# A convolution and squared-ReLU feed-forward kernel: new loads, a split first convolution and a new order in blocks 0 to 3

## The chip, the cores and the metric

One core of one Trainium2 chip. The metric is device time in microseconds (us) of one execution. The engines are called TensorE (PE in the profile; PEld is its weight load), VectorE (DVE), ScalarE (ACT), GpSimd (POOL) and SyncE (SP).

## The reference, cut to what matters

```python
# x: (8, 4096, 192), weight_gen: (8, 4096, 8 heads, 7 taps)
w = exp(weight_gen - max); w = w / sum(w)          # softmax over the 7 taps
out[b, s, head] = sum_k w[b, s, head, k] * x_pad[b, s + k, head]   # causal, 24 channels a head
h = maximum(out.reshape(32768, 192) @ w_in, 0)     # w_in (192, 2048)
return (h * h) @ w_out                             # w_out (2048, 192)
```

Everything is float32 outside; the kernel computes in float16 with float32 sums.

Of the kernel before, what the change touches and what calls it, by code (L numbers as in the profile page):

```python
# [9 lines left out]
def kernel(  # L10
# [7 lines left out]
):  # L18

# [38 lines left out]
    SL = 8  # L58
# [33 lines left out]
    mask = const.tile([P, P, 2], f16, name="mask")  # L92
    FIRST = 8
# [4 lines left out]
    ]  # L98

    def band_mask():  # L100

        nc.gpsimd.memset(mask, 1.0)
        for sign, base in ((1, 0), (-1, KK - 1)):
            nc.gpsimd.affine_select(
                out=mask, in_=mask, pattern=[[sign, P], [0, 2]], compare_op=AluOp.is_ge,
                fill=0.0, base=base, channel_multiplier=-sign,
            )

# [14 lines left out]

    def cross_w_in(q):
        for r0, r1 in ((0, RT), (RT, 0)):
            nc.sync.dma_start(out=w_i[r0 : r0 + RT, q, 1], in_=w_i[r1 : r1 + RT, q, 0])

# [10 lines left out]
    def load_w_out(q, n):  # L138
        nc.gpsimd.dma_start(
            out=w_o[:, q * NF // n : (q + 1) * NF // n],  # L140
            in_=moe_w_out[q * Dff // n : (q + 1) * Dff // n].rearrange(
                "(c p) m -> p c m", p=P
            ),
        )
# [139 lines left out]
    def x_load_f32(j):  # L284
        x_st[j] = p_one.tile([P, (R + HALO) * HK], f32, name="x_st", tag="ex")
        block_load(
            j, x_st[j][:, 0 : NT * D].rearrange("p (t d) -> p t d", t=NT), x[j // NBB], D, nc.sync
        )

    def x_cast(j, copy):  # L290
        x_t[j] = p_x.tile([P, NT, D], f16, name="xt")
        copy(out=x_t[j].rearrange("p t d -> p (t d)"), in_=x_st[j][:, 0 : NT * D])
# [6 lines left out]
    def wr_load_sbuf(j, parts, order, engines):  # L299

        wr_t[j] = p_wr.tile([P, NT, HP, SL * 2], f16, name="wr")
# [46 lines left out]
    def conv_pieces(j):  # L348


        s0, n = BLOCKS[j]
        th = n * TB // 2
        halves = []
        for half in (0, 1):
            s, a = (s0 + half, 0) if n == 2 else (s0, th * half)
            halves.append([
                (s, i, half, max(bounds[i], a), min(bounds[i + 1], a + th), a)
                for i in range(NT) if bounds[i] < a + th and bounds[i + 1] > a
            ])
        if n == 2:  # L360
# [14 lines left out]
    def st_conv(j):  # L375

        n = BLOCKS[j][1]
        th = n * TB // 2
        per = 1024 // th
        y = p_y.tile([P, NK, TB], f16, name="y")  # L380
        y_t[j] = y
# [3 lines left out]
        for later, s, i, q, half, a, b, base in conv_pieces(j):  # L385
# [7 lines left out]
            col = th * (k % per) - base  # L393
# [9 lines left out]
        for n, yp in enumerate(yps):  # L403
            k0, k1 = n * per, min((n + 1) * per, NK)
            nc.scalar.copy(  # L405
                out=y[:, k0:k1, 0:th],
                in_=yp[:, 0 : (k1 - k0) * th].rearrange("p (k c) -> p k c", c=th),
            )

    def st_unit(j, u):  # L410

        th = BLOCKS[j][1] * TB // 2
        per = TB // th
        h = ps_h.tile([P, 2, TB], f32, name="h", tag="h")
        for jj in range(per):
            for slot in range(NK):
                for half, r0 in enumerate((0, RT)):
                    k = slot ^ half if slot < 2 else slot
                    nc.tensor.matmul(  # L419
                        out=h[:, half, jj * th : (jj + 1) * th],  # L420
                        lhsT=w_in_chunk(u * per + jj, slot, half),
                        rhs=y_t[j][r0 : r0 + RT, k, 0:th],
                        start=(jj == 0 and slot == 0), stop=(slot == NK - 1),
                        skip_group_check=True,
                        tile_position=(r0, 0),
                    )
# [3 lines left out]
        g_t[(j, u)] = g  # L430
# [4 lines left out]
    def new_o(pool, banks=2):  # L435
        if pool is ps_o:
            return [ps_o.tile([P, TB], f32, name=f"o{i}") for i in range(banks)]
# [3 lines left out]
    def st_mm2(j, qt, fcs, ccs, o):  # L441


        th = BLOCKS[j][1] * TB // 2
        per = TB // th
        half, off = divmod(qt * QT, th)
        for fc in fcs:
            g = g_t[(j, fc // per)][:, half, fc % per * th + off :]
            for cc in ccs:
                n = P // len(o)  # L450
                for i, oo in enumerate(o):
# [3 lines left out]
                        lhsT=g[r0 : r0 + n, cc * P : (cc + 1) * P],  # L455
# [32 lines left out]
    with nc.allow_low_precision("fp16 matmul pipeline"), tc.manual_schedule():  # L488
# [18 lines left out]
        warm = const.tile([P, TB], f16, name="warm")  # L507
        nc.vector.memset(warm, 0.0)  # L508
# [3 lines left out]
        wp = ps_h.tile([P, 2 * TB], f32, name="wp", tag="h")  # L512

        def spin(n):
            for i in range(n):
                nc.tensor.matmul(  # L516
                    out=wp[:, 0:TB], lhsT=warm[:, 0:P], rhs=warm, start=True, stop=True
                )

        s0, s1, s2 = parts[:3]  # L520
        spin(42)
        band_mask()
        s0.load(nc.sync)
# [3 lines left out]
        ]  # L527
        load_w_in(w_st[0], 0, nc.sync)
        x_load_f32(0)
        load_w_in(w_st[1], 1, nc.sync)  # L530
        s0.exp(0, s0.rh)
# [3 lines left out]
        nc.scalar.copy(out=w_i[:, 0, 0], in_=w_st[0])  # L535
        wr_load_sbuf(0, [s0], (0, 2, 1, 4, 3), (nc.sync, nc.gpsimd))
        wr_load_sbuf(1, [s0], range(NT), (nc.gpsimd,))
        cross_w_in(0)
        x_cast(0, nc.scalar.copy)
        x_load_f32(1)  # L540
        nc.scalar.copy(out=w_i[:, 1, 0], in_=w_st[1])
        cross_w_in(1)
        s1.load(nc.sync)
        for i in (0, 2, 1, 3, 4):
            st_band(0, (i,))
        st_conv(0)
        st_bands(1)
        x_cast(1, nc.vector.tensor_copy)

        nc.gpsimd.memset(x_st[1][:, 0:1], 0.0)  # L550
# [3 lines left out]
        nc.gpsimd.memset(v_big, 0.0)  # L554
# [3 lines left out]
        orders = {0: "uuuuuCuuu", 1: "MuMuuuMuuuMCu", 2: "MuuuuMuuuuMuuuuuuuMCu"}  # L558
        steady = "MuMuuu" * 3 + "MuuuMCu"

# [4 lines left out]
        def at(j, u, kind, *args):  # L565
# [5 lines left out]
            (0, 2): ((1, 7), (2, 0)),  # L571
            (0, 3): ((2, 15), (3, 0)),
# [8 lines left out]
        def exp_time(j, u):  # L581

            if u == 0:
                return j - 1, 5 if j == 2 else 12
            return j, {1: 0, 7: 3, 9: 4, 15: 8}[u]

        at(0, 4, "exp", s1, 0, s1.rh)
        at(0, 5, "soft", s1, 0, s1.rh)
        for n, s in enumerate(parts[2:], 2):
# [5 lines left out]
            pieces = [(lo, min(lo + PIECE, s.rh)) for lo in range(0, s.rh, PIECE)]  # L595
            for (j, u), (lo, hi) in zip(times, pieces, strict=True):
                at(*exp_time(j, u), "exp", s, lo, hi)
                at(j, u, "soft", s, lo, hi)
            if n > 2:
                at(times[0][0] - 1, 0, "load", s)  # L600
        for j in range(1, NBLK - 1):
            a = BLOCKS[j + 1][0]
            small = [p for p in parts if p.fb <= j + 1][-1].r == FIRST
            us = {1: (1, 3), 2: (6, 8), 6: (7, 9)}.get(j, (5, 9) if small else (1, 5))
            for n, u in enumerate(us):
                at(j, u, "band", a + n)
# [14 lines left out]
        def run_fill(j, u):  # L621
            for kind, *args in fill.get((j, u), ()):
                if kind == "band":
                    st_bands(*args)
                    continue
                if kind == "load":
                    args[0].load(nc.sync)
                    continue
                s, lo, hi = args
                if kind == "exp":  # L630
                    s.exp(lo, hi)
                    continue
                s.total(lo, hi)
                s.recip(lo, hi)
                s.scale(lo, hi, nc.vector)
                if hi < s.rh:
                    continue
                if s.r == FIRST:
                    move_rows(s)
                    after = parts[parts.index(s) + 1]  # L640
                    if after.b == s.b and after.r > FIRST:
                        s.store(nc.sync)
                else:
                    s.store(nc.sync)
                    stored.add(s)
                    for w in [w for w in waiting if w[0] is s]:
                        waiting.remove(w)
                        load_rows(w[1])

        FCS = (range(NF // 2), range(NF // 2, NF))  # L650
        for j, (sub, n) in enumerate(BLOCKS):
            if j + 2 < NBLK:
                load_rows(j + 2)
            u = m = 0
            for step in orders.get(j, steady):
                if step == "M":
                    qt, part = divmod(m, 2)
                    m += 1
                    if part == 0:
                        o = new_o(ps_o, 1 if j < 3 else 2)  # L660
                    st_mm2(j - 1, qt, FCS[part], (0, 1), o)
                    if part == 1:
                        o_sum(j - 1, qt, (0, 1), o)
                        if qt % 2:
                            o_store(j - 1, qt - 1, range(4), nc.sync)
                elif step == "u":
                    run_fill(j, u)
                    st_unit(j, u)
                    u += 1
                elif j + 1 < NBLK:  # L670
                    st_conv(j + 1)
            if j == 0:
                x_load(2)
                x_load(3)
            elif j < NBLK - 2:
                for k in range(BLOCKS[j + 2][0], sum(BLOCKS[j + 2])):
                    x_load(k)
# [47 lines left out]
```

## The kernel before: what the change and the argument touch

The 32768 rows are worked through in blocks: two of 512 rows (blocks 0 and 1), then 31 of 1024. In each block the convolution is done on TensorE with banded weights `bd` (made by VectorE from softmax rows `wr` and a mask), ScalarE copies the result to `y`, 8 or 16 *units* follow (TensorE `h = w_in.T y`, ScalarE relu to `t`, VectorE square to `g`), and half-quarters *M* of the second product, four or eight a block, are placed between the units of the next block. A plan gives each block's order: `u` a unit, `M` a half-quarter, `C` the next block's convolution.

```python
orders = {0: "uuuuuCuuu", 1: "MuMuuuMuuuMCu", 2: "MuuuuMuuuuMuuuuuuuMCu"}
steady = "MuMuuu" * 3 + "MuuuMCu"
```

The start, shortened:

```python
spin(42)                                  # warm-up matmuls
s0.load(nc.sync)                          # softmax weights of the first 1024 rows
load_w_in(w_st[0], 0, nc.sync); x_load_f32(0); load_w_in(w_st[1], 1, nc.sync)
s0.exp(...); s0.total(...); s0.recip(...); s0.scale(...)
nc.scalar.copy(out=w_i[:, 0, 0], in_=w_st[0])           # cast of the first half of w_in
wr_load_sbuf(0, [s0], (0, 2, 1, 4, 3), (nc.sync, nc.gpsimd))   # band rows of block 0
wr_load_sbuf(1, [s0], range(NT), (nc.gpsimd,))
cross_w_in(0)        # a transfer: partition halves swapped, a second copy of w_in
x_cast(0, nc.scalar.copy); x_load_f32(1)                # x of block 1
nc.scalar.copy(out=w_i[:, 1, 0], in_=w_st[1]); cross_w_in(1)
s1.load(nc.sync)                                        # the second softmax weights
... bands, st_conv(0) ...
for q in range(4): load_w_out(q, 4)   # "(c p) m -> p c m": rows of 768 bytes
```

The softmax here doesn't subtract the row's maximum and nothing guards it: scores larger than these inputs give would overflow.

## Time and profile before

| | before |
|---|---|
| time, median (lowest to highest) | 751.77 us (751.57 to 751.93), 3 runs |
| span of the profiled execution | 749.2 us |
| first conv matmul, first relu | 12.29, 16.34 us |
| chain of waits on TensorE for good but for small pieces | from 63.28 us |
| last matmul ends | 745.86 us |

A group of the profile's timeline reads: start, length, engine, source line, operation, output<-input, shape, count, and in brackets how long the engine was idle before it and who ended that. The lines themselves stand in the prediction.

### The profile page before, as it was taken

The page shows a single profiled execution, that of the slowest core. Times are in us where ns is not written, and L with a number is a line of the kernel's source. Part 1 is how long each engine was busy: PE and PEld are TensorE (multiplying, and loading weights), DVE is VectorE, ACT ScalarE, POOL GpSimd, SP SyncE. Part 2 cuts the span into 40 slices and gives each one's busy share as a digit, 9 for nine tenths or more (in the row PEclk, how much of TensorE's full clock was granted, in tenths as well). Part 3 has the DMA queues.
Part 4 walks back from the last instruction along what each step waited for, and adds up shares of the span by engine and source line. Part 5 has one row for each costly group of instructions (what it writes and reads, how often), then busy time and mean ns, then how long its engine had stood idle before and what let it go on. Part 6 is the DMA issues. An engine that isn't in the chain of part 4 may idle for free.

```text
span 749.2 us, 33282 instructions
## 1 busy us (share of the span) xinstructions
PE 739.0 (99%) x15106; PEld 559.8 (75%) x15106; DVE 621.8 (83%) x1001; ACT 623.0 (83%) x753; POOL 87.9 (12%) x127
## 2 busy tenths in 40 slices
PE   8899999999999999999999999999999999999998
PEld 4658777777887777777877777777778777777787
DVE  5889998998789888887888888898888987677853
ACT  4898888888888888888888888888888888888883
POOL 3522220001101000011000110001100011001000
PEclk9999999999999999999999999999999999999999
DMA  8846444446453344543245442365441354441312
GB/s 231 129 74 135 79 68 109 101 78 138 93 109 69 74 77 80 131 86 65 46 80 139 86 80 49 55 138 108 59 79 47 57 109 80 59 75 50 50 45 65
DMA packets 122329, 65.20 MB, mean 87 GB/s; under 512 B 83881, under 2 KB 118668, under 8 KB 121676
## 3 DMA queue, kind: packets, MB, share of 16 engines
q1 hardware_dynamic: 77868, 46.05, 22.4%
q0 software_dynamic: 44176, 16.93, 20.6%
q8 instruction: 118, 1.93, 1.1%
q14 instruction: 23, 0.19, 0.1%
q10 hardware_dynamic: 144, 0.10, 0.0%
HBM read 48.61 MB, written 28.70 MB: 103 GB/s over the span
## 4 chain that ended last, share of the span: by engine, by line
PE 88%; DVE 5%; DMA 3%; ACT 1%; issue 1%; SPq 0%; POOL 0%; DVEq 0%; ACTq 0%
PE o L453 42%; PE h L419 40%; PE yp L394 6%; DVE g L431 2%; DVE bd L326 1%; DMA xt<-in_x_dram 1%; ACT t L428 1%; DMA x_st<-in_x_dram 1%; DMA vd<-v_big 1%; DVE v_first L217 1%; DVE ssum L202 0%; DVE rcp L209 0%; DMA wg<-in_weight_gen_dram 0%; DVE o_sb L469 0%; POOL wr L308 0%
## 5 line engine op out<-in xcount | busy, mean ns | idle before, releaser
L428 ACT ACTIVATE t<-h 128x1024 f16<-128x1024 f32 x512 | 497.1, 1027 | 66.9 <-PE h L419 66.6
L431 DVE TENSOR_TENSOR g<-t 128x1024 f16<-128x1024 f16 x512 | 334.5, 687 | 101.9 <-ACT t L428 99.1
L453 PEld LDWEIGHTS <-g 64*128 64x128 f16 (+1 forms) x8032 | 353.0, 94 | 55.7 <-issue 5.0
L453 PE MATMUL o<-w_o,g 64*128 64x192 f16 (+1 forms) x8032 | 386.1, 243 | 1.7 <-DMA w_o<-in_moe_w_out_dram 0.7
L419 PE MATMUL h<-y,w_i 64*128 64x512 f16 (+1 forms) x3168 | 379.8, 370 | 2.1 <-ACT t L428 0.9
L419 PEld LDWEIGHTS <-w_i 64*128 64x128 f16 x3168 | 165.5, 94 | 114.7 <-issue 5.0
L326 DVE TENSOR_TENSOR bd<-wr,mask 128x4160 f16<-128x4160 f16 (+3 forms) x89 | 149.4, 1702 | 4.6 <-DMA wr<-v_first 4.6
L278 POOL DMA_DIRECT2D xt<-in_x_dram x62 | 51.3, 832 | 446.1 <-PE yp L394 422.8
L467 ACT COPY o_sb<-o 128x384 f32<-128x384 f32 x129 | 62.3, 483 | 33.2 <-PE o L453 33.2
L469 DVE TENSOR_TENSOR o_sb<-o,o_sb 128x384 f32<-128x384 f32 x123 | 68.2, 554 | 8.0 <-ACT o_sb L467 5.6
L405 ACT CAST y<-yp 128x1024 f16<-128x1024 f32 (+1 forms) x64 | 48.2, 803 | 16.5 <-PE yp L394 16.5
L394 PE MATMUL yp<-bd,xt 128*32 128x104 f16 (+8 forms) x3864 | 52.0, 208 | 1.8 <-DMA xt<-in_x_dram 1.2
L394 PEld LDWEIGHTS <-xt 128*32 128x32 f16 (+3 forms) x3864 | 46.1, 91 | 8.0 <-issue 6.4
L217 DVE TENSOR_TENSOR v_big<-ex,rcp 128x112 f16<-128x112 f32 (+1 forms) x136 | 27.3, 263 | 1.8 <-DMA vd<-v_big 0.6
L195 ACT ACTIVATE ex<-wg 128x448 f32<-128x448 f32 (+2 forms) x44 | 27.2, 618 | 1.9 <-DMA wg<-in_weight_gen_dram 1.9
L202 DVE TENSOR_REDUCE ssum<-ex 128x64 f32<-128x448 f32 (+2 forms) x44 | 26.1, 593 | 2.4 <-ACT ex L195 2.4
L209 DVE RECIPROCAL rcp<-ssum 128x64 f32<-128x64 f32 (+2 forms) x44 | 23.7, 539 | 1.5
L268 POOL DMA_DIRECT2D xt<-in_x_dram x7 | 3.8, 547 | 136.9 <-PE yp L394 136.9
L308 POOL DMA_DIRECT2D wr<-v_first x31 | 16.8, 562 | 15.4 <-DVE v_first L217 15.3
L516 PE MATMUL wp<-warm 128*128 128x512 f16 x42 | 11.1, 432 | 1.3 <-DVE warm L508 1.3
L516 PEld LDWEIGHTS <-warm 128*128 128x128 f16 x42 | 4.5, 109 | 7.4 <-issue 2.5
L217 DVE TENSOR_TENSOR v_first<-ex,rcp 128x112 f16<-128x112 f32 (+1 forms) x48 | 9.1, 255 | 0.3
(19 smaller groups left out, 24.5 us busy)
## 6 DMA issues: line engine op xcount, KB each, us to landing
out_dram<-o_sb SPq DMA_DIRECT2D x63, 384.0 KB, 2.9
xt<-in_x_dram POOLq DMA_DIRECT2D x42, 240.0 KB, 6.0
wg<-in_weight_gen_dram SPq DMA_DIRECT2D x4, 1064.0 KB, 7.7
xt<-in_x_dram POOLq DMA_DIRECT2D x20, 192.0 KB, 5.6
wr<-vd SPq DMA_DIRECT2D x38, 80.0 KB, 5.0
vd<-v_big SPq DMA_DIRECT2D x5, 512.0 KB, 5.5
wg<-in_weight_gen_dram SPq DMA_DIRECT2D x5, 392.0 KB, 4.2
wg<-in_weight_gen_dram SPq DMA_DIRECT2D x3, 616.0 KB, 5.5
```

The costliest lines, as they stand in the source:

```text
L195: nc.scalar.activation(out=self.ex[:, lo:hi].rearrange("p r g k e -> p (r g) k e"), in_=self.wg[:, lo:hi].rearrange("p r (g e) k -> p (r g ...
L217: eng.tensor_tensor(out=bass.AP(tensor=v.tensor, offset=v.offset + lo * H * SL + lo % SL * 2 + g * SL * 2, ap=[list(v.ap[0]), [H * SL + 2, ...
L278: eng.dma_start(out=dst[:, first:last], in_=ap)
L326: nc.vector.tensor_tensor(out=bd_t[j][:, H * lo : H * (lo + len(tiles) * n)].rearrange("p (g m c) -> p g m c", g=shape[1], c=2 * SL), in0= ...
L394: nc.tensor.matmul(out=yps[k // per][p0 : p0 + m, col + a : col + b], lhsT=x_t[s][:, i, 32 * q : 32 * q + m], rhs=bd[:, h // 2, h % 2, a - ...
L405: nc.scalar.copy(out=y[:, k0:k1, 0:th], in_=yp[:, 0 : (k1 - k0) * th].rearrange("p (k c) -> p k c", c=th),)
L419: nc.tensor.matmul(out=h[:, half, jj * th : (jj + 1) * th], lhsT=w_in_chunk(u * per + jj, slot, half), rhs=y_t[j][r0 : r0 + RT, k, 0:th], ...
L428: nc.scalar.activation(out=t1, in_=h, func=ActF.Relu)
L431: nc.vector.tensor_tensor(out=g, in0=t1, in1=t1, op=AluOp.mult)
L453: nc.tensor.matmul(out=oo[:, cc * Dm : (cc + 1) * Dm], lhsT=g[r0 : r0 + n, cc * P : (cc + 1) * P], rhs=w_o[r0 : r0 + n, fc, :], start=(fc ...
L467: nc.scalar.copy(out=o_sb, in_=o[0][:, c])
L469: nc.vector.tensor_tensor(out=o_sb, in0=o[1][:, c], in1=o_sb, op=AluOp.add)
```

## The change

Its intent is an earlier and denser start. Its parts, in a diff cut to its core:

```diff
-        spin(42)
+        spin(25)
+        half_swap()
         s0.load(nc.sync)
         load_w_in(w_st[0], 0, nc.sync)
-        x_load_f32(0)
+        x_load_f32(0, x_st2, 0)
         load_w_in(w_st[1], 1, nc.sync)
+        x_load_f32(1, x_st2, 1)           # queued at once
+        s1.load(nc.sync)                  # queued at once
 ...
-        nc.scalar.copy(out=w_i[:, 0, 0], in_=w_st[0])
+        cast_w_in(0, w_st[0])             # reads every fourth float32
 ...
-        cross_w_in(0)
+        cross_w_in_by_pe(0)               # 3 matmuls with a permutation, 2 VectorE copies
+        spin(14)
 ...
+    def cast_w_in(q, src):
+        nc.scalar.copy(
+            out=w_i[:, q, 0].rearrange("r (g c p) -> r g c p", c=4, p=P),
+            in_=src.rearrange("r (g p c) -> r g c p", c=4, p=P))
 ...
     def load_w_out(q, n):
-                "(c p) m -> p c m", p=P
+                "(p c) m -> p c m", p=P    # rows of 3 KB
 ...
-        st_conv(0)
+        st_conv(0, 0)                      # first 256 rows; the rest is step "c"
+        nc.gpsimd.tensor_copy(out=gate, in_=x_st[1][:, 0:1])   # w_out waits for x of block 1
         for q in range(4):
             load_w_out(q, 4)
 ...
-        orders = {0: "uuuuuCuuu", 1: "MuMuuuMuuuMCu", 2: "MuuuuMuuuuMuuuuuuuMCu"}
+        plans = {
+            0: "B1 u X1 c u E1 S1 u u u C u M u u",
+            1: "L3 u B2 B3 u u M u u u E2 u E2 S2 M S2 C u M",
+            2: "L4 u u u u M u u u u B4 M B5 u E3 u M u u u u S3 M u E3 C u",
+            3: "L5 L6 S3 M u u u M u u u u M M B6 u u u u E4 M M B7 u u E4 u M u C S4 M u",
+        }
```

`B` makes a block's bands, `E` and `S` are the ScalarE and VectorE parts of a softmax, `L` its load, `X` a cast of x. In block 0 the first four units take 128 columns of four chunks each, so they can start on the first half of the convolution. From block 4 on the order is the old one.

## The prediction

The two VectorE copies of the swap were counted as free, and a unit of 128 columns as no longer than ScalarE's 0.95 us. The "ring" is the row of transfers that SyncE has asked for; that it is worked off in order was an assumption. The 0.31 MB/us is what the kernel before moved from 5 to 9.7 us (313 GB/s), and the 0.65 us of three matmuls agrees with its warm-up (32 in 6.79 us).

> **What bounds the kernel now.** I read the page first, then busy time by stretch, the chain of waits, the timeline of the first 65 us, and the DMA view.
>
> The page's first lines: one row per engine (busy us, share of the span, instructions), then the span in 40 slices.
>
> ```profile
> PE 739.0 (99%) x15106; PEld 559.8 (75%) x15106; DVE 621.8 (83%) x1001; ACT 623.0 (83%) x753; POOL 87.9 (12%) x127
> ...
> PE   8899999999999999999999999999999999999998
> ```
>
> TensorE is full from the third slice on. The chain of waits, in order of time (start us, length us, what), says where it becomes the bound:
>
> ```profile
> 0.81 3.19 DMA wg<-in_weight_gen_dram
> ...
> 8.37 0.64 SPq L308
> ...
> 12.24 5.13 DMA x_st<-in_x_dram
> 17.38 0.03 issue
> 17.41 0.02 DVEq L292
> 17.43 0.04 issue
> 17.47 0.66 DVE xt L292
> ...
> 63.28 1.48 PE o L453 x31
> ```
>
> Up to 63.28 us the chain wanders between loads, VectorE and ScalarE; from there to 745.86 it is TensorE but for a stretch at 117 to 142 us in which TensorE itself loses only about half a microsecond, and two gaps of 0.3. The steady double block repeats in 22.5 us (conv 1.50 + 16 units of 0.647 + 8 half-quarters of the second product of 1.32) and the change doesn't touch it. So only two things can be gained: time before the first convolution, and TensorE's gaps up to 63 us. I size the gaps with the spacings where TensorE is full: a 256-column h matmul 51.7 ns, a 512-column one 107.8, a K=128 o matmul 82.5, a K=64 one 41.2, a conv matmul 13.3. Work done by 63.28: four convs 4.9, 16 units of 256 columns 9.9, 124 matmuls of 512 columns 13.4, 8 M of 16 matmuls 10.6 and 2 M of 32 2.6 = 41.4 us. Hence 21.9 us are lost: 12.3 before the first conv matmul, about 9.6 after it. (Other losses: 3.3 us of tail after the last matmul, which stays.)
>
> The timeline shows where those 9.6 go (start us, length us, engine, instruction, in brackets the idle before it and its releaser):
>
> ```profile
> 11.49 2.60 DVE L326 TENSOR_TENSOR bd<-wr,mask 128x832 f16<-128x832 f16 x5 [3.15 <-DMA wr<-v_first]
> ...
> 14.62 0.80 ACT L405 CAST y<-yp 128x768 f16<-128x768 f32 x1 [1.93 <-PE yp L394]
> ...
> 16.34 3.77 ACT L428 ACTIVATE t<-h 128x1024 f16<-128x1024 f32 x4 [0.92 <-PE h L419]
> ...
> 24.14 1.48 PE L453 MATMUL o<-w_o,g 128*128 128x192 f16 x16 [0.72 <-DMA w_o<-in_moe_w_out_dram]
> ...
> 36.65 1.58 PE L394 MATMUL yp<-bd,xt 128*32 128x104 f16 x118 [1.05 <-DMA xt<-in_x_dram]
> ```
>
> From 12.3 to 23.2 TensorE does 6.9 us of work in 10.9: lost 4.0. Then it waits for w_out, 1.0 with the pipeline's restart, for the squares behind the second softmax, 0.7, for x at the third convolution (35.0 to 36.65), 1.6, and 1.0 in the seven units in a row at 48.6. Why it can't simply catch up shows in busy time by stretch (stretch, its length, then busy us and count of PE, PEld, DVE, ACT, POOL):
>
> ```profile
> 16.30:25.30 9.00, 7.32 (x172) 6.19 (x168) 7.14 (x16) 8.95 (x10) 6.14 (x7) 1.00 1.03 162
> 25.30:28.20 2.90, 2.80 (x34) 1.84 (x34) 2.90 (x8) 1.02 (x1) 2.08 (x4) 1.00 0.50 143
> 28.20:39.00 10.80, 9.56 (x237) 7.88 (x238) 9.73 (x15) 8.63 (x12) 3.36 (x6) 1.00 0.70 133
> 39.00:59.10 20.10, 19.82 (x314) 12.38 (x316) 17.73 (x31) 19.15 (x24) 6.14 (x11) 1.00 0.43 74
> ```
>
> ScalarE is busy 8.95 of 9.00 and 19.15 of 20.10 us in the first and last of these: in blocks 0 to 2 a unit costs it 0.95 us against TensorE's 0.62 to 0.65, with few M between. **From the first relu (16.34) to the last relu of block 2 (59.13) ScalarE is the bound**, with 37.75 us of work and 5.0 of idle. VectorE is close behind.
>
> [...] the first wr issued from SyncE at 8.37 landed at 11.44, just after w_in's second half, queued before it, landed at about 11.2; but one from GpSimd took as long. [...] here the engines are 98% busy at 302 GB/s from 5 to 10 us. [...] a concurrent pair of h matmuls here takes 215.7. [...]
>
> **The change part by part.**
>
> *Loads queued at once.* x of block 1 (0.49 MB) and the second softmax's weights (0.40 MB) now stand on SyncE's ring directly behind w_in. Removes the 5.13 us wait at 12.24. But they also stand ahead of the two wr pieces (tiles 0 and 2) that SyncE issues at 8.4: 0.89 MB at 0.31 MB/us is 2.8 us. Bulk that drains at about 9.7 now drains at 12.5, and with 1.5 us to landing (9.7 to 11.2 before) the wr pieces land at about 14.2 instead of 11.5, if the ring is kept in order.
>
> *Conv in two parts.* The first part needs bands 0 to 2, 1.75 us, not five, 2.6; 36 matmuls; its y copy has 384 columns, by the 0.80 of 768 about 0.48. From wr landing to the first relu: three bands 1.75, last conv pieces 0.4, y 0.55, first unit 0.6 = 3.2 us, against 4.85 before (11.49 to 16.34). Gain 1.6. It adds one y copy of 0.48 to ScalarE within the bound stretch. Units of 128 columns are 24 matmuls[...].
>
> *Swap by TensorE.* Three 512-column matmuls, 0.65 us, in place of warm-up, and two VectorE copies of 1024 and 512 fp32[...]. They lie at 9 to 11 us, where VectorE idles 3.15 us for wr: free. The crossing transfer of 0.38 MB goes from the ring; it was hidden behind the y copy.
>
> *w_out in 3 KB rows, issued once x of block 1 has landed.* From 18.75 to about 13 to 14 us; before, the GpSimd queue held 98% of all engines from 18 to 26 us with 768-byte rows. Landed by 20, before the first M: saves the 1.0.
>
> *Order.* x of block 2 is asked for after the second conv part and x of block 3 one conv later: the 1.6 us at the third convolution goes. The half-quarters are spread between units, and o alternates between two banks in blocks 0 and 1.
>
> Sum, by the bound of blocks 0 to 2: first relu at 14.2 + 3.2 = 17.4; ScalarE's work 37.75 + 0.48; of its 5.0 idle some 3.3 belong to w_out, to x and to the second softmax in the way, so 1.7 stay. End of block 2's relus: 17.4 + 38.2 + 1.7 = 57.3 against 59.13: **1.8 us gained**. VectorE gives a check: about 46 us of work from the first band to 63.3, with 5.8 idle; begun at 14.2 it can't end before 60.2, so at most 3.1 gained. Add a few tenths for the wait at 62.9 (0.4).
>
> **The rivals.**
> *A: the ring doesn't hold wr back.* For it: GpSimd's and SyncE's wr landed alike, and the pieces are 16 KB. Then wr lands at 11.5, the first relu at 14.7, and 4.5 us are gained: 747.3, and with the tenths and a tighter order 746.
> *B: it holds wr back and the order merely moves the waits.* Bands 2 and 3 now stand together early in block 1, 4.7 us of VectorE ahead of seven squares, with five t buffers; the second softmax (3.3 us) stands before the third square. If ScalarE waits for t buffers there, nothing is gained: 751 to 752.
> *C: all gaps go.* If the ring isn't kept and ScalarE never idles: 1.7 + 5.0 - 0.5 = 6.2 us, 745.5. TensorE would then do 41.4 us of work from 12.2 to about 57, still 3.4 lost, so it is not impossible.
>
> **Range and chances.** I give the ordered ring 0.6 (about 749.5), A and C together 0.3 (746), B 0.1 (751.5); the mean is 748.6. That the order is written step by step to fit these waits speaks for its working, so I say 748.0 us, from 744.8 to 751.0. Faster by 2% needs 15 us; all loss before 63 us is 21.9, of which the first load (4.0), softmax (4.3) and wr (3) take 11.3 that no part shortens: chance 0.01. Slower by 2%: 0.01. Within: 0.98.
>
> **What would show it.** In the profile after: the first band at about 14.2 (rival A: 11.5); the first relu at 17.4 (A: 14.7); no wait for w_out before the first M and none for x at the third convolution; from the first relu to block 2's last ScalarE idle under 2.5 us; from about 61 us on the chain TensorE's alone, at the same 22.5 us per double block. I am wrong if block 3 and later run slower, if the first wr lands early, or if ScalarE idles for t buffers in block 1.

## The result, and the profile after

The changed kernel takes **755.19 us** (754.10 to 756.56, 4 runs) against 751.85 (751.57 to 753.22, 4 runs) of the kernel before: 0.4% slower, ratio 1.0042 with an interval of 1.0021 to 1.0062. It lies outside the predicted range. A ratio here is the mean time of one kernel's runs over that of the other's of the same rounds, so it isn't quite the ratio of the medians quoted.

The changed kernel's page, engines and TensorE's slices:

```profile
PE 740.8 (98%) x15178; PEld 550.1 (73%) x15178; DVE 624.1 (83%) x1003; ACT 626.7 (83%) x754; POOL 87.1 (12%) x128
```

```profile
PE   7799999999999999999999999999999999999998
```

The work is the same to within 2 us on TensorE (740.8 against 739.0); only the first two slices are emptier. Its chain of waits (start, length, what):

```profile
2.37 5.57 DMA w_st<-in_moe_w_in_dram
...
12.29 4.27 DMA wr<-v_first
...
20.45 1.22 PE h L471 x37
21.67 3.69 issue
25.36 2.08 PE h L471 x23
```

It goes through the loads and wr, then through TensorE with a hole of 3.69 us; the last stretch away from TensorE that is worth naming is at 77.8 to 86.0 us. The timeline (same columns as before):

```profile
8.04 2.91 ACT L138 CAST w_i<-w_st 128x1536 f16<-128x1536 f32 x1 [3.07 <-DMA w_st<-in_moe_w_in_dram]
...
15.54 4.87 DVE L358 TENSOR_TENSOR bd<-wr,mask 128x832 f16<-128x832 f16 x7 [1.89 <-DMA wr<-v_first]
...
17.59 0.48 ACT L449 CAST y<-yp 128x384 f16<-128x384 f32 x1 [1.71 <-PE yp L438]
...
19.00 1.02 ACT L480 ACTIVATE t<-h 128x1024 f16<-128x1024 f32 x1 [0.94 <-PE h L471]
...
20.45 1.22 PE L471 MATMUL h<-y,w_i 64*128 64x128 f16 x37 [0.17 <-ACT y L449]
...
25.36 2.08 PE L471 MATMUL h<-y,w_i 64*128 64x128 f16 x23 [3.69 <-issue]
```

Three things are new. The first band starts at 15.54 us, where it was 11.49, and the first relu at 19.00, where it was 16.34. The cast of w_in takes 2.91 us, where it took 1.47 (the line below, of the kernel before). And TensorE stops for 3.69 us after the 37th of a run of unit matmuls, *in the middle of a unit of 24*, with "issue" as its releaser: it waited for nothing that the profile shows.

```profile
7.24 1.47 ACT L535 CAST w_i<-w_st 128x1536 f16<-128x1536 f32 x1 [2.28 <-DMA w_st<-in_moe_w_in_dram]
```

Busy time by stretch in the changed kernel (stretch, length, busy us and count of PE, PEld, DVE, ACT, POOL, then TensorE's granted clock, DMA share, GB/s):

```profile
12.00:13.00 1.00, 1.00 (x4) 0.43 (x3) 1.00 (x2) 0.05 (x1) 0.00 (x0) 0.50 1.08 358
...
22.00:23.00 1.00, 0.00 (x0) 0.00 (x0) 0.98 (x2) 1.00 (x2) 0.00 (x0) 1.00 1.03 258
...
25.00:26.00 1.00, 0.64 (x13) 0.64 (x14) 1.00 (x5) 0.00 (x0) 0.16 (x1) 0.50 0.09 11
```

TensorE does nothing from 22 to 23 us while the DMA engines are full (1.03), and after its two long stops, of 2.62 and 3.69 us, it is granted half its clock (0.50), at 12 and at 25 us. Before, the clock was 1.00 in every microsecond of the first 30.

The convolutions show how the loss grows. The profile of the changed kernel is of its slowest execution (756.56 us), that of the kernel before of a fast one (751.43), so the table ends at 5.4 us where the medians differ by 3.3. A convolution that in the changed kernel has one M fewer ahead of it is shifted by the 1.32 us of an M:

| start of conv of block | before, us | after, us | equal work later by |
|---|---|---|---|
| 0 | 12.29 | 16.45 | 4.2 |
| 1 | 19.28 | 27.37 | 8.1 |
| 2 (its bulk) | 36.65 | 40.01 + 1.32 | 4.7 |
| 3 | 55.50 | 60.41 | 4.9 |
| 4 | 78.41 | 81.62 + 1.32 | 4.5 |
| 5 | 100.96 | 106.42 | 5.5 |
| last matmul ends | 745.86 | 751.23 | 5.4 |

So 4.2 us are lost before the first convolution, another 3.9 between it and the second, 3.4 are won back in the next stretch, and from block 5 on nothing changes any more. Why the start, and why the stop?

### The profile page after: what moved, and what is told of

Its sections match the earlier page's. It is cut to its first block, busy times and chain, and to the rows that moved or that the text cites. A ratio compares the mean times of both kernels' runs of the same rounds, so it can differ in the third digit from the quotient of the medians.

```text
span 754.6 us, 33431 instructions
## 1 busy us (share of the span) xinstructions
PE 740.8 (98%) x15178; PEld 550.1 (73%) x15178; DVE 624.1 (83%) x1003; ACT 626.7 (83%) x754; POOL 87.1 (12%) x128
## 3 DMA queue, kind: packets, MB, share of 16 engines
q8 instruction: 118, 1.93, 1.0%
## 4 chain that ended last, share of the span: by engine, by line
PE 94%; DVE 2%; issue 1%; DMA 1%; ACT 1%; SPq 0%; ACTq 0%; DVEq 0%
PE o L507 44%; PE h L471 43%; PE yp L438 6%; DMA w_st<-in_moe_w_in_dram 1%; DVE g L487 1%; DMA wr<-v_first 1%; DVE bd L358 1%; ACT t L480 0%; ACT w_i L138 0%; ACTq L340 0%; ACT xt L323 0%; DVE o_sb L523 0%; ACT y L449 0%; ACT o_sb L521 0%; DVE v_first L248 0%
## 5 line engine op out<-in xcount | busy, mean ns | idle before, releaser
L507 PEld LDWEIGHTS <-g 64*128 64x128 f16 (+1 forms) x8032 | 347.1, 94 | 59.3 <-issue 4.9
L507 PE MATMUL o<-w_o,g 64*128 64x192 f16 (+1 forms) x8032 | 381.1, 243 | 1.3 <-DVE o_sb L523 0.6
L471 PE MATMUL h<-y,w_i 64*128 64x512 f16 (+2 forms) x3216 | 376.1, 368 | 5.2 <-issue 4.3
L471 PEld LDWEIGHTS <-w_i 64*128 64x128 f16 x3216 | 156.0, 94 | 123.7 <-issue 7.2
L449 ACT CAST y<-yp 128x512 f16<-128x512 f32 (+2 forms) x65 | 48.3, 792 | 14.7 <-PE yp L438 14.6
L571 PE MATMUL wp<-warm 128*128 128x512 f16 x39 | 11.6, 467 | 1.3 <-DVE warm L563 1.3
```

The costliest lines, as they stand in the source:

```text
L449: nc.scalar.copy(out=y_t[j][:, k0:k1, col0 : col0 + w], in_=yp[:, 0 : (k1 - k0) * w].rearrange("p (k c) -> p k c", c=w),)
L471: nc.tensor.matmul(out=h[:, half, jj * w : (jj + 1) * w], lhsT=w_in_chunk(fc, slot, half), rhs=y_t[j][r0 : r0 + RT, k, col : col + w], sta ...
L507: nc.tensor.matmul(out=oo[:, cc * Dm : (cc + 1) * Dm], lhsT=g[r0 : r0 + n], rhs=w_o[r0 : r0 + n, fc, :], start=(fc == 0 and cc == ccs[0]), ...
```

## The experiments

Theory 1: the start waits for the rows `wr`, which are held back by the loads now queued ahead of them. Theory 2, a rival: the strided cast delays the start. For the stop, theory A: TensorE's own instructions came late, behind other transfers (the page has a DMA queue "instruction", of 118 pieces); theory B: a wait on data that the profile doesn't show. Theory C: the halved clock (0.50) after the idle stretches, the first of which has 25 warm-up matmuls before it where the kernel before runs 42 without a stop, costs part of the time (the run tests the first stretch only). Twelve experiments follow, in the order of three batches and a last single run; "the change" is the changed kernel, and each edit is against it unless said otherwise. All gave correct results. Each batch has its own runs of the kernel before: 751.88 us in the median for the first, 752.03 for the second, 752.1 for the third, 752.69 for the last.

### Plain cast and 768-byte rows again (a_rows)

```diff
-            out=w_i[:, q, 0].rearrange("r (g c p) -> r g c p", c=4, p=P),
-            in_=src.rearrange("r (g p c) -> r g c p", c=4, p=P),
+            out=w_i[:, q, 0],
+            in_=src,
-                "(p c) m -> p c m", p=P
+                "(c p) m -> p c m", p=P
```

> The change with w_out in rows of 768 bytes again and so the cast of w_in without strides. Theory 1 (the start waits for the band rows wr, held back by the loads queued before them): both casts fall from 2.92 us to 1.47, the swap moves forward by 1.5 us, but the first band stays near 15.5 us and the first relu near 19.0; time within 1 us of the change's 755.2. Theory 2 (the strided cast delays the start): first relu 1.5 to 3 us earlier, time 752 to 753.5.

Measured: 752.66 us (752.27 to 753.02), ratio 1.0011 (0.9994 to 1.0028). The casts take 1.47 us. The first band starts at 15.92 and the first relu at 20.05 us, no earlier than in the change: theory 2 falls for the start. Yet 2.5 us are won, which theory 1 had not expected: the time lies where theory 2 put it, for another reason. The timeline says where:

```profile
23.70 1.15 PE L471 MATMUL h<-y,w_i 64*128 64x128 f16 x23 [0.99 <-issue]
```

The stop, at the same point of the program, is 0.99 us in place of 3.69. With the rows of w_out the stop changed.

### x and second weights asked for after the first wr (a_queue)

```diff
-        x_load_f32(1, x_st2, 1)
-        s1.load(nc.sync)
         s0.exp(0, s0.rh)
 ...
         wr_load_sbuf(0, [s0], (3, 4), (nc.gpsimd,))
+        x_load_f32(1, x_st2, 1)
+        s1.load(nc.sync)
```

> The change with the loads of x of block 1 and of the second softmax's weights asked for after the first block's wr, not before. Theory 1: first band at about 11.6 us in place of 15.5, first relu at 15 to 15.5 (the second cast of w_in, 2.9 us from about 11.3, then holds ScalarE to 14.2); time 751 to 752.5. Theory 2 (strided cast): first relu hardly moves, time 754.5 to 755.5.

Measured: 750.75 us (750.18 to 751.20), ratio 0.9985 (0.9970 to 1.0000): 4.4 us less than the change. wr lands in the median 3.7 us after its issue, not 5.9, and the first band starts with no wait at all, but at 13.71 us, not at the expected 11.6:

```profile
11.97 1.82 DVE L157 CAST w_i<-pt 128x1024 f16<-128x1024 f32 x2 [3.71 <-PE pt L153]
13.71 4.39 DVE L358 TENSOR_TENSOR bd<-wr,mask 128x832 f16<-128x832 f16 x6
```

The two copies of TensorE's swap stand before the bands in VectorE's order, the swap waits for the strided cast (2.1 us in this run), and so the cast is now on the path. First relu at 17.24. The stop at the old place is gone; one of 1.25 us comes later, at 24.96. So the 4.4 us aren't the price of the late wr alone: the first relu moved by 1.76 us, and the stop of 3.69 went with it.

### Third weights and x of block 2 later (a_late)

```diff
         for q in range(4):
             load_w_out(q, 4)
-        s2.load(nc.gpsimd)
 ...
                     st_conv(0, 1)
-                    x_load(2)
 ...
                     if j == 0:
+                        s2.load(nc.gpsimd)
+                        x_load(2)
                         x_load(3)
```

> The change with the third softmax part's weights and x of block 2 asked for after the convolution of block 1. Theory A (TensorE's 3.7 us stop at 21.7 us, in the middle of a unit and with no wait, is the next piece of its instructions coming late behind the transfers that GpSimd queued): the stop shrinks to under 1.5 us, the low clock at 25 to 28 us goes, time 751.5 to 753. Theory B (it is a wait on data that the profile doesn't show): stop 3.7 us as before, time 755.

Measured: 754.95 us (753.80 to 756.87), ratio 1.0044: no gain, a miss. The time is the one that theory B expected. In its profile the stop is 2.51 us, at the same matmul, which is what neither theory expected; and as this profile is of the fastest execution and the changed kernel's of the slowest, the 1.2 us between the two stops need not be the edit's. w_out and the crossing of w_in's second half alone still keep the engines eight to nine tenths busy up to 21.2 us.

### More warm-up matmuls (a_spin)

```diff
-        spin(25)
+        spin(37)
 ...
-        spin(14)
+        spin(24)
```

> The change with 37 and 24 warm-up matmuls in place of 25 and 14, so 22 matmuls and 22 weight loads more stand before the first unit. The warm-up is then long enough that the clock doesn't fall at 11 to 15 us. Theory A (late instructions): the stop falls at the same count of instructions from the program's start, so 22 matmuls earlier in the units. Theory B (data): at the same matmul. Theory C (the low clock of 11 to 15 us costs the time): time 753 or less; otherwise within 1 us of 755.2.

Measured: 756.39 us (755.16 to 757.38), ratio 1.0060. The granted clock is 1.00 from 8 to 16 us, and nothing is won: theory C falls for the first of the two low stretches. What the clock alone is worth there isn't measured, since the longer warm-up also held the first convolution to 17.19 us, from 16.45. The second stretch stayed (0.73 in the mean of 24 to 28 us), and no run tests it alone. And the timeline decides between A and B:

```profile
20.77 0.60 PE L471 MATMUL h<-y,w_i 64*128 64x128 f16 x15 [0.17 <-ACT y L449]
...
25.37 2.85 PE L471 MATMUL h<-y,w_i 64*128 64x128 f16 x45 [4.00 <-issue]
```

The stop comes after the 15th matmul of that run, not after the 37th: exactly the 22 matmuls earlier that were added in front. A wait on data would have stayed with its matmul. **The stop hangs on the count of instructions from the start of TensorE's program.** The matmuls counted in the other profiles say the same: wherever TensorE stops with "issue" in the first 60 us, in ten profiles in all, it has done exactly 223, 351 or 607 matmuls since its start, whatever the work there. Two of these counts, from the busy time up to the end of the stop (PE comes first, its count after the x), in the change and in a_queue:

```profile
0.00:25.30 25.30, 16.93 (x223) 8.41 (x224) 16.23 (x34) 13.52 (x11) 12.62 (x23) 0.93 0.90 212
...
0.00:26.10 26.10, 20.51 (x351) 11.86 (x352) 18.79 (x39) 17.03 (x15) 14.74 (x27) 1.00 0.85 208
```

The three counts are 128 or 256 apart, and with one weight load a matmul, 128 matmuls are 256 instructions. The page's DMA part fits: its "instruction" queue moved 118 pieces, 1.93 MB, and TensorE has 15178 matmuls and as many weight loads; if the pieces are all TensorE's, that is an estimated 64 bytes an instruction and some 257 instructions a piece, which agrees with the distance of the counts. Read in narrow windows, the first piece ran at 22.7 to 22.8 us in the change, 21.75 to 22.0 in a_late, 21.25 to 21.5 in a_rows, 22.5 to 22.75 here, and TensorE went on at 25.36, 24.27, 23.70 and 25.37: each time 2.2 to 2.9 us after the piece. In the kernel before it ran at 15.2 us, and there is no such stop. When it ran, TensorE had done 114 matmuls in the kernel before, 98 in a_queue, 186 in a_rows, and all 223 in the change, a_late and a_spin.

### Both undone (a_rq)

The edits of a_rows and a_queue together.

> The change with both undone: w_out in 768-byte rows with the plain cast, and x of block 1 and the second weights asked for after the first wr. If wr is held by the loads and, once it isn't, by the strided cast (through the swap and the two copies that stand before the bands on VectorE): first band at 11.6 to 12.3 us, first relu at 14.5 to 15, time 748 to 749.5. If the strided cast costs nothing: first band at 13.7 and 750.7 as with the order of loads alone.

Measured: 749.23 us (747.73 to 751.35), ratio 0.9968 (0.9943 to 0.9993). First band at 12.12, first relu at 15.59 us, 0.75 before that of the kernel before. So without the strided cast the bands start 1.6 us earlier than in a_queue. With both undone, what is left of the change (conv in two parts, swap by TensorE, new order) is worth 2.4 us of the means against the kernel before. The profiled execution was the slowest of the four (751.35): it waits 0.9 us for w_out in the first M, and has two stops of 0.5 and 0.6.

### Both undone and less traffic (a_rql)

The edits of a_rq and a_late together.

> As a_rq, and the third part's weights and x of block 2 asked for after the convolution of block 1. If TensorE's stops come from instructions fetched behind GpSimd's transfers, no stop over 0.7 us is left before 30 us and the time falls by 0 to 1.2 us against a_rq; if x of block 2 then comes too late for its convolution, that costs 0.5 to 1 us and the two are alike.

Measured: 749.78 us (749.00 to 751.74), ratio 0.9977 (0.9955 to 1.0000). Its profile has no stop before 30 us, as expected. No difference in time from a_rq can be told.

### First half of w_in crossed by transfer (a_rqs)

```diff
+        cross_w_in(0)
         x_load_f32(1, x_st2, 1)      # against a_rq
 ...
-        cross_w_in_by_pe(0)
-        spin(14)
+        spin(17)
```

> As a_rq, but the first half of w_in is crossed by transfer again, as in the kernel before, not by TensorE. If TensorE's swap is worth having, the first unit waits for the crossing (0.38 MB behind wr, landed at about 14) and x of block 1 comes 1.2 us later: 0.3 to 1.5 us slower than a_rq. If it only moved hidden work: equal within 0.5 us.

Measured: 750.25 us (748.88 to 750.65), ratio 0.9976 (0.9957 to 0.9996) beside 0.9968 of a_rq in the same rounds. The first relu falls at 16.84, 1.25 us later than in a_rq. The times differ by 0.08%, less than the runs can tell: TensorE's swap is worth a microsecond at the start; what is left of it in the end these runs can't tell.

### The kernel before with 3 KB rows and strided cast alone (b_rows)

```diff
-        nc.scalar.copy(out=w_i[:, 0, 0], in_=w_st[0])    # against the kernel before; w_st[1] likewise
+        nc.scalar.copy(
+            out=w_i[:, 0, 0].rearrange("r (g c p) -> r g c p", c=4, p=P),
+            in_=w_st[0].rearrange("r (g p c) -> r g c p", c=4, p=P),
+        )
-                "(c p) m -> p c m", p=P
+                "(p c) m -> p c m", p=P
```

> The kernel before with one part of the change alone: w_out in 3 KB rows and the strided cast that this needs. The casts take 2.92 us in place of 1.47 (on the way to the first y copy: the second one ends about 1.5 to 2.9 us later, so the first relu moves from 16.3 to 17 to 18.5), the first M waits for w_out less by 0 to 0.7. Time 752 to 754 if the cast costs more than the rows give; 751 to 751.9 if not.

Measured: 750.76 us (749.90 to 754.76), ratio 1.0004 (0.9969 to 1.0039): nothing to tell. Both casts take 2.97 us, but the second ends at 14.2, just before the first y copy at 14.69, and the first relu stays at 16.41, against the expected 17 to 18.5. The cast is a cost only where its end is waited for.

### The two loads from GpSimd's queue (a_pool)

Against a_rows:

```diff
-        x_load_f32(1, x_st2, 1)
-        s1.load(nc.sync)
+        x_load_f32(1, x_st2, 1, nc.gpsimd)
+        s1.load(nc.gpsimd)
```

> As a_rows (plain cast, 768-byte rows), with the loads of x of block 1 and of the second weights at the same early place, but queued by GpSimd, so that nothing new stands on SyncE's ring before the first wr. If wr was held by the order of SyncE's ring: its wr lands at 11.5 to 12.3 us, as when the loads come later, and the first relu falls at 15 to 15.5. If it is held by all that is in flight at the time, whatever the queue: wr lands at 14 to 16 us and the first relu is at 18 to 20.

Measured: 752.60 us (751.06 to 753.77), ratio 0.9997 (0.9969 to 1.0026). Nothing new stands on SyncE's ring before its first wr, and yet this is the view of the tile wr for that single transfer, issued at 8.2 us, and what it took to land:

```profile
L340 SPq DMA_DIRECT2D wr<-v_first x1: 637/637/637, 8.2 to 8.2; - x1
...
DMA to landing us min/median/max: 8.1/8.1/8.1
```

It lands at 16.3 us; the first band starts at 16.44, the first relu at 20.57. **The order of SyncE's ring isn't what holds wr: with the two loads in flight from another queue it took 8.1 us to land, where in the kernel before a wr took 2.7 in the median.**

### The end of block 3 in the steady order (a_rql_tail)

```diff
-            3: "... B7 u u E4 u M u C S4 M u",     # against a_rql
+            3: "... B7 u u E4 u M u M C S4 u",
```

> As a_rql, with the end of block 3 put back to M, M, conv, softmax, u as in the steady order. The changed kernel takes 24.8 us from the conv of block 4 to that of block 5, with one M more in it than before, which needs 22.55 + 1.32 = 23.87, so 0.9 us are lost there on the o banks. Put back: 22.6 us for that stretch and 0.5 to 1.0 us less in all than a_rql: 748.5 to 749.3. If the loss only moves: equal to a_rql.

Measured: **748.40 us** (747.33 to 750.93, 6 runs), ratio 0.9952 (0.9930 to 0.9974): the fastest kernel, faster than the kernel before and the change, though it can't be told from the next. What this edit alone adds to a_rql (0.9977 in another batch) isn't clear of noise either. From conv of block 4 to conv of block 5 it takes 22.55 us (78.25 to 100.80), as the kernel before does. Its profile is again of the slowest execution, with 2.15 us of wait for w_out before the second half of the first M.

### The old order (a_rq_old)

```diff
-            0: "B1 u X1 c u E1 S1 u u u C u M u u",     # against a_rq
-            1: "L3 u B2 B3 u u M u u u E2 u E2 S2 M S2 C u M",
-            ...
+            0: "B1 u X1 c u E1 S1 u u u C u u u",
+            1: "L3 M u M B2 u u E2 B3 u M u E2 u u M C S2 u",
+            2: "L4 M S2 u u u u M u u B4 u u M B5 E3 u u u u E3 u u u M C S3 u",
+            3: "L5 L6 M S3 u M u u u M u M B6 u u u M E4 u M B7 u u u M E4 u u u M C S4 u",
```

> As a_rq, but blocks 0 to 3 in the order of the kernel before (M, softmax parts and bands where they were), with the two-part conv and TensorE's swap kept. If the new order is worth having: 0.5 to 2 us slower than a_rq's 749.2. If its gain is undone by what it loses at the start of blocks 4 and 5: within 0.5 us of a_rq, or faster.

Measured: 749.09 us (747.77 to 751.50, 6 runs), ratio 0.9957 (0.9936 to 0.9978), with a_rq at 0.9968 in another batch. The new order as it stands gains nothing that these runs can show.

### 3 KB rows without the strided cast (a_step)

Against a_rql_tail, with the rows of 3 KB; the columns are picked when weights are loaded:

```diff
-        return w_i[RT * half : RT * (half + 1), q, part, col : col + P]
+        return w_i[RT * half : RT * (half + 1), q, part, col : col + 4 * P].rearrange(
+            "r (p c) -> r c p", c=4
+        )[:, f % 4]
```

> As a_rql_tail, but w_out in 3 KB rows again, with the plain cast of w_in: the reordering of its columns is left to the weight loads of the first product, which read every fourth column. If such a weight load takes as long as one of neighbouring columns (94 ns, two of them per 82 to 216 ns of a matmul pair), the first M's wait for w_out (2.1 us in a_rql_tail's profile) falls under 0.8 and the time is 747 to 748.4. If it takes longer than about 108 ns each, the pairs of h matmuls no longer hide it and all 31 blocks grow: over 755 us.

Measured: 749.75 us (749.07 to 751.74, 6 runs), ratio 0.9966 (0.9947 to 0.9986). The group of weight loads of the first product (busy us, mean ns, then idle before):

```profile
L473 PEld LDWEIGHTS <-w_i 64*128 64x128 f16 x3216 | 177.2, 111 | 102.6 <-issue 3.0
```

A load of every fourth column takes 111 ns (94 for neighbouring columns in the changed kernel), over the 108 that I had set as the limit (by the 107.8 ns from one 512-column h matmul to the next), and still 18 h matmuls take 1.94 us in the chain of waits, as before: the loads stay hidden. The wait for w_out before the first M is gone; a wait of 1.6 us for x of block 2 stands in its place. The time isn't under that of a_rql_tail; in different batches the two can't be told apart.

## Why the prediction was wrong

**What bounds the kernel: right.** From block 5 on, equal work stays 5.4 to 5.5 us later to the end: the start decides all. ScalarE's work from the first relu to the last of block 2 was put at 38.2 us; it is 38.69, in the busy time of the changed kernel. (The prediction's 124 matmuls of 512 columns before 63.28 us are 120 in the trace, 0.4 us less work; nothing rests on it.) The line:

```profile
19.00:64.27 45.27, 40.88 (x836) 30.03 (x834) 38.86 (x68) 38.69 (x47) 11.86 (x19) 0.96 0.48 96
```

**Loads queued at once: right in direction, wrong in mechanism and size.** The step "the wr pieces land at about 14.2 instead of 11.5, if the ring is kept in order" failed. They gave the first band at 15.54. The ring's order isn't the cause (a_pool, where the two loads are off SyncE's ring and wr lands later still, 8.1 us after its issue). How the bytes in flight delay a piece of 16 KB the runs don't show. A second piece is SyncE's own waits, which I hadn't looked for: its DMA queue's waits in the changed kernel include these (waiter, what it waited for, us in total, times, longest).

```profile
SPq L340 <- DMA w_st<-in_moe_w_in_dram: 1.9, 1, 1.9
SPq L303 <- DMA w_st<-in_moe_w_in_dram: 1.3, 1, 1.3
```

So x of block 1 was issued at 7.05, not 5.8, and the second wr at 11.28. Why SyncE waits there for an earlier load to land the trace doesn't say; "queued at once" didn't hold for all of them. Undoing this part alone is worth 4.4 us of the medians, the stop's part in them included.

**From wr to the first relu: right.** Worked out as 3.2 us, measured 15.54 to 19.00, 3.46. A unit of 128 columns takes TensorE 0.85 us (24 matmuls, at 18.12), less than ScalarE's 1.02 for its relu.

**Swap by TensorE: wrong in "free".** The two copies took 1.22 and 0.68 us. They are free in the change, where VectorE waits 1.89 us for wr after them anyway; in a_queue they hold the bands, to 13.71.

**w_out in 3 KB rows: a term of the sum was missing.** I took the change of layout as a matter of the transfer and gave the cast that it needs no cost. Reading every fourth float32 (16 bytes apart), it took 2.92 us for 1.47. The part's gain, w_out before the first M, came true in the change (no such wait in its profile), as did the end of the wait for x at the third convolution.

**Not foreseen: the stop.** The step "end of block 2's relus: 17.4 + 38.2 + 1.7" holds no term for it. The relus end at 64.27, not 57.3; 1.6 of the 7.0 come from the later first relu, 0.5 from more work, and 4.9 from ScalarE's idle time, 6.6 us where I allowed 1.7. Of that, 3.12 stand directly before the first relu after the stop; in the low clock that follows (0.50 from 25 to 28 us, 0.83 to 29) the 23 matmuls after the stop take 2.08 us, and in a_rows 1.15. That the stop is instructions coming late is supported by a_spin (it moves with the instruction count, 22 matmuls), by the counts of 223, 351 and 607, and by the like time from piece to restart (2.2 to 2.9 us). That other transfers delay the piece is supported by a_rows (0.99) and a_rql (none) and by the count at which the first piece ran, not proved: the trace has no time at which a piece is asked for. w_out may be the transfer that counts: in the change, a_spin, a_late, a_pool and a_rows, with stops of 0.99 to 4.00 us at the 223rd matmul, it was asked for at 13.56 to 14.59 us, before the first piece ran; in the rest at 15.79 or later, and of these only a_rqs (1.05) stopped there for over 0.61 us. No run moves w_out alone. Why 3 KB rows delay the piece more than 768-byte rows stays open; the rows alone don't, as a_step has them and no stop in its first 60 us.

**The gain of the order: wrong.** I let "3.3 of its 5.0 idle" go. In the change, 3.4 us are won back from conv 1 to conv 2, which looks like it; but in part this is the other engines' lead from the stop. In a_rq, without the big stop, the same stretch wins 1.2 (19.83 to 34.68, plus 1.32, is 16.2, against 17.4), the relus of block 2 end at 58.86, and ScalarE's idle from the first relu is about 5, as before. In a_rq_old the old order does as well. The new one also loses 0.9 us at the seam of blocks 3 and 4, where an M, one unit and an M follow each other and the last must wait until VectorE has added up the two banks of o, as the changed kernel's timeline has it:

```profile
86.06 1.48 PE L507 MATMUL o<-w_o,g 64*128 64x192 f16 x31 [0.60 <-DVE o_sb L523]
```

a_rql_tail, which puts the seam back, removes it in the trace. Of the rivals, B came nearest in kind, but its cause, t buffers, was not it: the one wait of ScalarE for VectorE that block 1 of the changed kernel shows is 0.37 us.

## What to carry to other kernels

When a load is moved earlier, ask what small, urgent transfer will now stand behind its bytes: here the urgent one took 5.9 us to land instead of 2.7 (medians), and 8.1 with the bulk on another queue. A new layout has a second end, so cost the copy that must match it (here 2.92 us for 1.47), and where the copy stands on its engine. And when an engine stops in the middle of uniform work with no releaser, shift its instruction count: if the stop moves along, as here by exactly 22 matmuls, it hangs on the engine's own program, not on data.
